# Projections mixed into attention as pairs of 64-row matmuls, with the value sums kept in SBUF between runs

## The chip, the cores and the metric

The kernel runs on one core of one Trainium2 chip, as one program. The metric is the device time of an execution in microseconds (us). PE is TensorE's matmul stream and PEld its weight loads, ACT is ScalarE, DVE is VectorE, POOL is GpSimd, SP issues the DMAs.

## What is computed

Two kinds of layer alternate, twice each, over 2048 tokens of width 576 with 32 heads of width 18:

```python
x = x + _A_ref(_layernorm(x), A_wq, A_wk, A_wv, A_wo)      # softmax attention, one key/value head
x = x + _B_ref(_layernorm(x), B_wqkv, B_w_phi, B_wo)       # linear attention on softmax features
...
# A: q per head, one k and one v for all heads
p = softmax(q @ k.T * Dh**-0.5);  o = p @ v;  return o @ wo
# B: phi = [softmax(t @ w_phi), softmax(-t @ w_phi)] for queries and keys, per head
kv = phi_k.T @ v;  z = phi_k.sum(tokens)
o = (phi_q @ kv) / (phi_q @ z + 1e-6);  return o @ wo
```

## The kernel before

Tokens stand in 16 tiles of 128, in four chunks of four tiles. Products of the projections are made in three parts from values split into a high and a low half (float32r): `PRODUCTS` (L232) lists 14 matmuls for each half of the 576 output columns (`HALF`, 288). `project` (L236) runs these 14 into one PSUM bank; it is a generator that gives way after every second matmul with a weight, and with a negative one after the last.

An attention layer (`attend`, L862) goes through 32 groups, a chunk of 512 queries with four heads each. For each of the 16 key tiles of a group, `score` (L503) makes scores in two *units* of two heads. The 56 rows of queries and keys of two heads lie in the two row halves of the array, so that a unit is a pair of 56-row matmuls (L504) with 512 columns into a score tile of two banks; there are three score tiles. ACT takes the exponential of a unit (L964, 128x1024) into one of nine `pt` tiles. `add_values` (L798) multiplies by the values: four matmuls, in four column strips of 32, per key tile (L800), summed over 16 key tiles in one PSUM bank. When a group is done, `finish_group` (L887) transposes that bank on DVE (`turned`, L889), normalizes (L895, L896), transposes back (L901), splits (L139, L140) and packs into `on` by DMA, in steps.

PSUM has eight banks: six for scores and two *homes* (L879), the tiles `ps` and `acc`. `homes[0]` is the accumulator of the group at hand; the other is `Spare`, in which mixed-in work runs. With each group they change places (L913).

Mixed-in work is the rest of layer A and the start of layer B for a chunk whose attention is done (`chunk_work`, L1206). Per tile: two output projections (`output`, L1048; the sum goes to the residual in `add_residual`, L294), then `flip_tokens` (L639: statistics, normalization and a DVE transpose, written out by DMA), and after the third tile `split_tokens` (L654). Then `mix` (L661) for each tile: two key and two value projections (`keys_values`, L555), two query projections (`queries`, L591), and `update_state` (L575), followed by `feature_end` (L545) for the queries and a block transpose (L632). After a key or query projection `feature_start` (L531) copies the sums to SBUF (L536), takes maximum, minimum and differences on DVE and the exponential on ACT (L543); after a value projection the sums are copied (L567) and `feature_end` follows for the keys. The last chunk's work is done after attention, with other banks (`Banks`, L1075).

The order is set by the loop at L1017. While mixed-in work is there (`bulk`):

```python
sums(scores(BURST))      # three units of scores, then the values that are ready
tick()
ready = scores(BURST)    # three more units
spent = fill()           # mixed-in work up to the next negative weight
in_order()
opens = units[2 * done[0]][1] == 0
if spent < HEAVY and not (spent and opens):
    sums(ready)          # not after a whole projection: that weighs 1750, HEAVY is 1500
tick()
tick()
```

`tick` (L926) takes one step of the finished groups, of the weight loads and of the slow transposes. `in_order` (L948) chains all instructions of PE and DVE in the order in which they were written, so both run exactly in program order. As `fill` stops right behind a projection's last matmul and what is done with its sums, whatever the generator does next (such as `flip_tokens`) is written in the following turn's `fill`, after that turn's values. Without mixed-in work the loop alternates two units and the values of one key tile.

Of the kernel before, what the change touches and what calls it, by code (L numbers as in the profile page):

```python
# [9 lines left out]
F32 = mybir.dt.float32  # L10
# [50 lines left out]
def kernel(ctx, tc, x_in, wq, wk, wv, wo, wqkv, w_phi, wob, out):  # L61
# [174 lines left out]
    def project(dst, w, c0, xs, after=None, products=range(len(PRODUCTS)), last=LASTP):  # L236
        for j, n in enumerate(products):
# [7 lines left out]
            elif j % 2:  # L245
                yield 250

    def run(gen):
        for _ in gen:
            pass  # L250
# [40 lines left out]
        lo_engine.tensor_sub(xs[64:P, 4, :], pb[64:P, :], xs[64:P, 4, :].bitcast(F32))  # L291
        yield -110

    def add_residual(i, b, po):  # L294
        xr = xres[i][:, b * HALF : (b + 1) * HALF]
        V.tensor_add(xr, xr, po)  # L296

    scratch = dram.tile([2, KT * P, D], F32, name="folded")
    flipped = dram.tile([TPC, D, P], F32, name="flipped")
# [228 lines left out]
                for j in range(2):  # L528
                    nc.sync.dma_start(dst[j], mp[:, j, :].bitcast(F32))

    def feature_start(src, e, b, copies):  # L531
        hi = small.tile([P, HH], F32, name="fmax")
        lo = small.tile([P, HH], F32, name="fmin")
        hs = slice(b * HH, (b + 1) * HH)
        if copies is V:
            V.tensor_copy(e[:, hs, 0, :], src)  # L536
# [18 lines left out]
    def keys_values(i, xs, e, st, ps, copies):  # L555
        vb = st["vb"][i % 2]
        for b in range(2):
            po = ps.tile([P, HALF], F32, name="ps")
            yield from project(po, st["wk"], b * HALF, xs, lambda: feature_start(heads(po), e, b, copies))

        def values(po, b):
            dst = vb[:, : H * (DH + 1)].rearrange("p (h d) -> p h d", d=DH + 1)
            dst = dst[:, b * HH : (b + 1) * HH, :DH]
            if copies is A:
                A.activation(dst, heads(po), AF.Copy)
            else:
                V.tensor_copy(dst, heads(po))  # L567
            feature_end(e, b, G if copies is A else V)

        for b in range(2):  # L570
            po = ps.tile([P, HALF], F32, name="ps")
            yield from project(po, st["wv"], b * HALF, xs, lambda: values(po, b))
        return vb

    def update_state(e, vb, st, ps, after=None):  # L575
# [14 lines left out]

    def queries(xs, e, st, ps, copies):  # L591
        for b in range(2):
            po = ps.tile([P, HALF], F32, name="ps")
            yield from project(po, st["wpq"], b * HALF, xs, lambda: feature_start(heads(po), e, b, copies))
        if copies is A:
            for b in range(2):
                feature_end(e, b, G)
# [145 lines left out]
    def read_out(i, pht, st, sp, ps):  # L743
        xo = sp.tile([P, 5 * P], F32, name="xo")
        xv = xo[:, :D].rearrange("p (h d) -> p h d", d=DH)
        for g0, g1 in ((0, 8), (8, NKG)):
            pn = ps.tile([P, 8 * NW], F32, name="ps")
            for g in range(g0, g1):
                hs = KG if g < NKG - 1 else 2
                for t0 in (0, 64):  # L750
                    T.matmul(pn[t0 : t0 + 64, (g - g0) * NW : (g - g0) * NW + hs * (DH + 1)],  # L751
                             pht[: 2 * DH * hs, g, t0 : t0 + 64],
                             st["kvb"][: 2 * DH * hs, g, : hs * (DH + 1)], start=True, stop=True)
            h0, h1 = g0 * KG, min(g1 * KG, H)
            nv = pn[:, : (h1 - h0) * (DH + 1)].rearrange("p (h e) -> p h e", e=DH + 1)
            den = small.tile([P, 24], F32, name="den")
            dv = den[:, : h1 - h0]
            V.tensor_scalar(dv, nv[:, :, DH], 1e-6, None, op0=ALU.add)
            V.reciprocal(dv, dv)
            V.tensor_mul(xv[:, h0:h1, :], nv[:, :, :DH], dv[:, :, None].to_broadcast([P, h1 - h0, DH]))  # L760
        V.tensor_copy(xo[:, D:], xo[:, 512:D])
        yield STAGE
        xs = sp.tile([P, 9, P], F32R, name="xs3")
        yield from transposed(xo, xs, ps, A)
        yield STAGE
        for b in range(2):
            po = ps.tile([P, HALF], F32, name="ps")
            yield from project(po, st["wob"], b * HALF, xs, lambda: add_residual(i, b, po))

    def next_queries(i, stats, layer, st, xpool, sp, ps):  # L770
        p, tt = divmod(i, PAIR)
# [71 lines left out]
    def last_group(acc, on, ps):  # L843
        with tc.high_priority():
            osb = bw.tile([P, 5 * P], F32, name="xn")[:, :CW]
            V.tensor_copy(osb, acc)
# [12 lines left out]
            split(parts[:, 0, :], parts[:, 1, :], osb, V, V)  # L859
            pack(on.bitcast(F32), parts.bitcast(F32), NG - 2)  # L860

    def attend(layer, st, a1o, extra, after_chunk, chunks):  # L862
# [13 lines left out]
        with ctx1:  # L876
# [7 lines left out]
            acc, on = {}, {}  # L884
            urgent, bulk, loads, slow = deque(), deque(), deque(), deque()

            def finish_group(c, g):  # L887
                turned = a1.tile([P, CW], F32, name="turned", bufs=2)
                V.transpose(turned, acc[c, g])  # L889
# [15 lines left out]
                for _ in range(3):  # L905
                    yield STAGE
                if g == NG - 2:
                    bulk.append(after_chunk(c, on[c], Spare(), loads, slow))
                yield STAGE

            def values(c, g, t, pt):
                if t == 0:
                    homes.reverse()  # L913
                    acc[c, g] = bank(*homes[0], [P, CW])
                add_values(acc[c, g], t, [pt[j // 2][:, j % 2, :] for j in range(GH)], t == 0, t == NT - 1)
                if t == NT - 1 and (c, g) == groups[-1]:
                    st["last"] = acc[c, g], on[c]
                elif t == NT - 1:
                    finish(c, g)

            def finish(c, g):
                f = finish_group(c, g)
# [45 lines left out]
            acc[groups[0]] = bank(*homes[0], [P, CW])  # L968
            at[0] = len(spots)
            done[0] = (at[0] - 2 * BURST) // 2  # L970

            def head_values(t, first, last):
                add_values(acc[groups[0]], t, [pts[0, t, j // 2][:, j % 2, :] for j in range(GH)], first, last)

            def head():
                for n, (unit, pt) in enumerate(zip(units, spots)):
# [71 lines left out]
    def output(c, tt, on, wpo, a1o, ps, copies):  # L1048
        xs = on[:, :, tt * P : (tt + 1) * P]
        for b in range(2):  # L1050
            po = ps.tile([P, HALF], F32, name="ps")
            yield from project(po, wpo, b * HALF, xs, lambda: add_residual(c * TPC + tt, b, po))

    def drain(queue):
        while queue:
# [111 lines left out]
    for layer in range(LAYERS):  # L1167
# [3 lines left out]
        with tc.tile_pool(name="a1o", bufs=2) as a1o:  # L1171
# [77 lines left out]
            for i in chunk_tiles(c):  # L1249
                tt = i - c * TPC  # L1250
                for b in range(2):
                    full = (i, b) not in sums
                    po = ps.tile([P, HALF], F32, name="ps") if full else sums[i, b]
                    run(project(po, st["wo"], b * HALF, on[:, :, tt * P : (tt + 1) * P],
                                None, (*EARLY, *LATE) if full else LATE, LATE[-1]))
                    add_residual(i, b, po)
                stats.update(ln_stats([i]))

        st["mixed"] = 0
# [71 lines left out]
```

## Time and profile before

| what | value |
|---|---|
| runs | 2699.45 to 2702.57 us, median of three 2701.58 |
| profiled execution, first to last instruction | 2699.8 us |
| PE busy | 2627.5 us (97%) |
| ACT busy | 2158.1 us (80%) |
| DVE busy | 1213.9 us (45%) |
| granted TensorE clock | 0.994 of full speed |

In the timeline a row gives start and length in us, engine, line, operation, output<-inputs, shape and how many instructions are merged into it; in brackets stands how long the engine was idle before it and what ended that. The groups by line give the count, busy us, the mean ns of one, then the idle time before them. A PE row's length holds the pipeline's latency, so the distance between starts is what one costs. Where a load's wait was over, the first matmul's row starts with its weight load.

### The profile page before, as it was taken

To read this page: it belongs to the slowest core of one execution; us is meant where nothing else is said; L and a number is where in the kernel's file an instruction comes from. 1 tells how busy PE (TensorE), PEld (TensorE's weight loads), DVE (VectorE), ACT (ScalarE), POOL (GpSimd) and SP (SyncE) were. 2 spreads that over 40 slices of the span, in tenths; PEclk is the share of its full clock that TensorE was granted. 3 is DMA by queue.
4 is the path that set the end of the run, shared out by engine and by line. 5 is a ranking of instruction groups with operands and counts; after the bars stand their busy time and mean duration, and the time that the engine had idled before them with its cause. 6 is when DMAs were issued, how large, how long until landed. Compare 5 with 4: busy or idle time off the path is not lost. (4 is left out here: it accounts for less than half of the span.)

```text
span 2699.8 us, 55195 instructions
## 1 busy us (share of the span) xinstructions
PE 2627.5 (97%) x22094; PEld 1444.8 (54%) x22094; DVE 1213.9 (45%) x2807; ACT 2158.1 (80%) x2551; POOL 75.6 (3%) x114
## 2 busy tenths in 40 slices
PE   7999999999999999999999999999999999999999
PEld 6633335453545454558996222455445544554788
DVE  8422244542454245437773111254525452545475
ACT  4599998999899989963335999999998999899421
POOL 1000000000000000002000000000000000000110
PEclk9999999999999999999999999999999999999999
DMA  6531254313421341136645210231224113412354
GB/s 184 163 121 54 65 166 153 93 28 86 119 49 35 84 122 45 38 97 193 185 134 177 71 28 23 55 111 38 58 73 117 41 32 99 118 36 71 108 162 136
DMA packets 353248, 254.30 MB, mean 94 GB/s; under 512 B 191770, under 2 KB 273882, under 8 KB 352986
## 3 DMA queue, kind: packets, MB, share of 16 engines
q1 hardware_dynamic: 352986, 250.71, 32.4%
q8 instruction: 176, 2.88, 0.5%
q14 instruction: 86, 0.70, 0.1%
HBM read 146.12 MB, written 83.69 MB: 85 GB/s over the span
## 5 line engine op out<-in xcount | busy, mean ns | idle before, releaser
L964 ACT ACTIVATE pt<-sc 128x1024 f32<-128x1024 f32 x2036 | 1915.9, 1112 | 155.9 <-PE sc L504 137.2
L504 PE MATMUL sc<-qst,kst 56*128 56x512 f32 x3840 | 712.6, 454 | 16.7 <-ACT pt L964 16.3
L504 PEld LDWEIGHTS sc<-qst,kst 56*128 56x128 f32 x3840 | 324.0, 184 | 618.1 <-ACT pt L964 573.9
L800 PE MATMUL acc<-pt,vst 128*32 128x512 f32 x4096 | 505.1, 599 | 0.0
L800 PE MATMUL ps<-pt,vst 128*32 128x512 f32 x4048 | 491.1, 600 | 1.4 <-DVE featk L536 1.4
L800 PEld LDWEIGHTS ps<-pt,vst 128*32 128x32 f32 x4048 | 105.7, 109 | 212.1 <-issue 206.4
L239 PE MATMUL ps<-wahi,xs 128*128 128x288 f32 x954 | 208.5, 305 | 0.9 <-ACT xs L137 0.7
L800 PEld LDWEIGHTS acc<-pt,vst 128*32 128x32 f32 x4096 | 103.3, 109 | 197.2 <-issue 191.5
L239 PEld LDWEIGHTS ps<-wahi,xs 128*128 128x128 f32 x954 | 157.6, 190 | 11.6 <-issue 3.9
L239 PE MATMUL ps<-walo,xs 128*128 128x288 f32 x530 | 156.2, 297 | 0.0
L889 DVE STREAM_TRANSPOSE turned<-acc 128x512 f32<-128x512 f32 x30 | 21.4, 714 | 217.5 <-PE acc L800 217.5
L388 PE MATMUL ps<-xsc,wbhi 128*128 128x256 f32 x576 | 107.7, 286 | 0.6 <-ACT xsc L137 0.6
L410 ACT ACTIVATE pc<-ps 128x256 fp32r<-128x256 f32 x80 | 30.4, 384 | 93.3 <-PE ps L388 89.2
L239 PEld LDWEIGHTS ps<-walo,xs 128*128 128x128 f32 x530 | 100.6, 190 | 0.0
L263 POOL TENSOR_TENSOR rstd<-var,neghalf 128x1 f32<-128x1 f32 (+1 forms) x56 | 32.0, 571 | 2439.9 <-DVE var L261 2417.7
L137 ACT ACTIVATE xs<-ps 128x512 fp32r<-128x512 f32 x40 | 23.8, 594 | 94.0 <-PE ps L282 93.9
L388 PEld LDWEIGHTS ps<-xsc,wbhi 128*128 128x128 f32 x576 | 91.5, 193 | 1.6 <-ACT xsc L137 1.1
L889 DVE STREAM_TRANSPOSE turned<-ps 128x512 f32<-128x512 f32 x32 | 22.9, 716 | 142.9 <-PE ps L800 142.9
L388 PE MATMUL ps<-xsc,wblo 128*128 128x256 f32 x320 | 86.1, 284 | 0.0
L239 PE MATMUL ps<-wchi,on 128*128 128x288 f32 x378 | 82.2, 303 | 0.0
L296 DVE TENSOR_TENSOR xc<-xc,ps 128x288 f32<-128x288 f32 x58 | 25.7, 445 | 123.4 <-PE ps L239 123.2
L536 DVE COPY featq<-acc 128x288 f32<-128x288 f32 x32 | 14.6, 457 | 123.0 <-PE acc L239 123.0
(257 smaller groups left out, 3200.8 us busy)
## 6 DMA issues: line engine op xcount, KB each, us to landing
qst<-qd SPq DMA_DIRECT2D x360, 72.0 KB
pht<-phi SPq DMA_DIRECT2D x32, 540.0 KB
qd<-pc SPq DMA_DIRECT2D x64, 256.0 KB
on<-parts SPq DMA_DIRECT2D x192, 72.0 KB
phi<-pht SPq DMA_DIRECT2D x96, 144.0 KB
wchi<-wod SPq DMA_DIRECT2D x35, 288.0 KB
wclo<-wod SPq DMA_DIRECT2D x35, 288.0 KB
wchi<-wpqd SPq DMA_DIRECT2D x35, 288.0 KB
```

The source lines that it names most:

```text
L137: A.activation(dst_hi, src, AF.Copy)
L239: T.matmul(dst, xs[:, slot, :], w[half][:, k, c0 : c0 + HALF], start=(n == 0), stop=(n == last))
L263: G.tensor_tensor(rstd, var, neghalf[:, :n], op=ALU.pow)
L296: V.tensor_add(xr, xr, po)
L388: T.matmul(po, lhs, xsc[:, slot, :], start=(n == 0), stop=(n == LASTP))
L410: A.activation(pc[:, 0, :], po, AF.Copy)
L504: T.matmul(sc, kst[head_rows(h), t * P : (t + 1) * P], q[head_rows(h), h // 2, :], start=True, stop=True)
L536: V.tensor_copy(e[:, hs, 0, :], src)
L800: T.matmul(acc[32 * j : 32 * j + 32, :], vst[:, t, :], pts[j], start=first, stop=last)
L889: V.transpose(turned, acc[c, g])
L964: A.activation(pt, sc, AF.Exp, scale=SCALE)
```

## The change

A projection in mixed-in work is made of pairs: for each of the 14 products a matmul over rows 0 to 63 into one bank and one over rows 64 to 127 into another. Both homes are used for this, the accumulator's first. Whoever takes up the sums reads both: a copy or an add of the first half, then an add of the second. So that the accumulator's bank is free, the first `sums` of each turn with mixed-in work ends with its *closing*: DVE copies or adds the bank to an SBUF tile `sum`, and the next values start a new sum in `homes[0]`. This goes on from the first chunk's output on (`started`). A finished group is summed from both places before it is transposed. The projections outside attention stay as they were.

```diff
+    def project_halves(dst, w, c0, xs, after):
+        for n, (slot, half, k) in enumerate(PRODUCTS):
+            for rows, part in ((slice(0, ROWT), dst[0]), (slice(ROWT, P), dst[1])):
+                T.matmul(part, xs[rows, slot, :], w[half][rows, k, c0 : c0 + HALF],
+                         start=(n == 0), stop=(n == LASTP))
+            if n == LASTP:
+                after()
+                yield -250
+            elif n % 2:
+                yield 250
+
+    def projected(ps, w, c0, xs, after):
+        if isinstance(ps, Banks):
+            po = ps.tile([P, HALF], F32, name="ps")
+            return project(po, w, c0, xs, lambda: after((po,)))
+        parts = ps.halves([P, HALF])
+        return project_halves(parts, w, c0, xs, lambda: after(parts))
...
-    def add_residual(i, b, po):
+    def add_residual(i, b, parts):
         xr = xres[i][:, b * HALF : (b + 1) * HALF]
-        V.tensor_add(xr, xr, po)
+        for po in parts:
+            V.tensor_add(xr, xr, po)
+
+    def gathered(dst, parts):
+        V.tensor_copy(dst, heads(parts[0]))
+        for po in parts[1:]:
+            V.tensor_add(dst, dst, heads(po))
...
         if copies is V:
-            V.tensor_copy(e[:, hs, 0, :], src)
             src = e[:, hs, 0, :]
+            gathered(src, parts)
+        else:
+            src = heads(parts[0])
...
-                V.tensor_copy(dst, heads(po))
+                gathered(dst, parts)
...
+                def halves(self, shape):
+                    return [bank(*home, shape) for home in homes]
...
             def finish_group(c, g):
                 turned = a1.tile([P, CW], F32, name="turned", bufs=2)
-                V.transpose(turned, acc[c, g])
+                a = acc.pop((c, g))
+                if a["sum"] is not None:
+                    V.tensor_add(a["sum"], a["sum"], a["bank"])
+                V.transpose(turned, a["bank"] if a["sum"] is None else a["sum"])
...
-            def values(c, g, t, pt):
+            def values(c, g, t, pt, closing):
                 if t == 0:
                     homes.reverse()
-                    acc[c, g] = bank(*homes[0], [P, CW])
-                add_values(acc[c, g], t, [pt[j // 2][:, j % 2, :] for j in range(GH)], t == 0, t == NT - 1)
-                if t == NT - 1 and (c, g) == groups[-1]:
-                    st["last"] = acc[c, g], on[c]
+                    acc[c, g] = {"bank": None, "sum": None}
+                a = acc[c, g]
+                opened = a["bank"] is None
+                if opened:
+                    a["bank"] = bank(*homes[0], [P, CW])
+                add_values(a["bank"], t, [pt[j // 2][:, j % 2, :] for j in range(GH)],
+                           opened, closing or t == NT - 1)
+                last = (c, g) == groups[-1]
+                if t == NT - 1 and last:
+                    st["last"] = a, on[c]
+                    closing = bool(bulk)
                 elif t == NT - 1:
                     finish(c, g)
+                    closing = False
+                if closing:
+                    if a["sum"] is None:
+                        a["sum"] = a1o.tile([P, CW], F32, name="sum", bufs=2)
+                        V.tensor_copy(a["sum"], a["bank"])
+                    else:
+                        V.tensor_add(a["sum"], a["sum"], a["bank"])
+                    a["bank"] = None
...
-            def sums(until):
+            def sums(until, close=False):
                 while done[0] < until:
                     n, t, _ = units[2 * done[0]]
-                    values(*groups[n], t, [pts.pop((n, t, hh)) for hh in range(2)])
+                    values(*groups[n], t, [pts.pop((n, t, hh)) for hh in range(2)],
+                           close and done[0] == until - 1)
                     done[0] += 1
                     in_order()
...
                 if bulk:
-                    sums(scores(BURST))
+                    sums(scores(BURST), started[0])
                     tick()
```

More of the change, by code (lines that the diff above doesn't have):

```diff
@@ L529, in exact_maxima, with feature_start @@
                     nc.sync.dma_start(dst[j], mp[:, j, :].bitcast(F32))
-    def feature_start(src, e, b, copies):
+    def feature_start(parts, e, b, copies):
         hi = small.tile([P, HH], F32, name="fmax")
@@ L557, in keys_values, with values @@
         for b in range(2):
-            po = ps.tile([P, HALF], F32, name="ps")
-            yield from project(po, st["wk"], b * HALF, xs, lambda: feature_start(heads(po), e, b, copies))
-        def values(po, b):
+            yield from projected(ps, st["wk"], b * HALF, xs, lambda parts: feature_start(parts, e, b, copies))
+        def values(parts, b):
             dst = vb[:, : H * (DH + 1)].rearrange("p (h d) -> p h d", d=DH + 1)
@@ L564, in values @@
             if copies is A:
-                A.activation(dst, heads(po), AF.Copy)
+                A.activation(dst, heads(parts[0]), AF.Copy)
             else:
-                V.tensor_copy(dst, heads(po))
+                gathered(dst, parts)
             feature_end(e, b, G if copies is A else V)
         for b in range(2):
-            po = ps.tile([P, HALF], F32, name="ps")
-            yield from project(po, st["wv"], b * HALF, xs, lambda: values(po, b))
+            yield from projected(ps, st["wv"], b * HALF, xs, lambda parts: values(parts, b))
         return vb
@@ L592, in queries @@
         for b in range(2):
-            po = ps.tile([P, HALF], F32, name="ps")
-            yield from project(po, st["wpq"], b * HALF, xs, lambda: feature_start(heads(po), e, b, copies))
+            yield from projected(ps, st["wpq"], b * HALF, xs, lambda parts: feature_start(parts, e, b, copies))
         if copies is A:
@@ L766, in read_out @@
         for b in range(2):
-            po = ps.tile([P, HALF], F32, name="ps")
-            yield from project(po, st["wob"], b * HALF, xs, lambda: add_residual(i, b, po))
+            yield from projected(ps, st["wob"], b * HALF, xs, lambda parts: add_residual(i, b, parts))
     def next_queries(i, stats, layer, st, xpool, sp, ps):
@@ L845, in last_group @@
             osb = bw.tile([P, 5 * P], F32, name="xn")[:, :CW]
-            V.tensor_copy(osb, acc)
+            if acc["sum"] is None or acc["bank"] is None:
+                V.tensor_copy(osb, acc["bank"] or acc["sum"])
+            else:
+                V.tensor_add(osb, acc["sum"], acc["bank"])
             po = ps.tile([P, TPC, P], F32, name="ps")
@@ L883, in tile @@
                     return bank(*homes[1], shape)
-            acc, on = {}, {}
+                def halves(self, shape):
+                    return [bank(*home, shape) for home in homes]
+            acc, on, started = {}, {}, [False]
             urgent, bulk, loads, slow = deque(), deque(), deque(), deque()
@@ L907, in finish_group @@
                 if g == NG - 2:
+                    started[0] = True
                     bulk.append(after_chunk(c, on[c], Spare(), loads, slow))
                 yield STAGE
-            def values(c, g, t, pt):
+            def values(c, g, t, pt, closing):
                 if t == 0:
                     homes.reverse()
-                    acc[c, g] = bank(*homes[0], [P, CW])
-                add_values(acc[c, g], t, [pt[j // 2][:, j % 2, :] for j in range(GH)], t == 0, t == NT - 1)
-                if t == NT - 1 and (c, g) == groups[-1]:
-                    st["last"] = acc[c, g], on[c]
+                    acc[c, g] = {"bank": None, "sum": None}
[9 more added lines that the diff above has]
+                    closing = bool(bulk)
                 elif t == NT - 1:
                     finish(c, g)
+                    closing = False
[3 more added lines that the diff above has]
+                        V.tensor_copy(a["sum"], a["bank"])
+                    else:
+                        V.tensor_add(a["sum"], a["sum"], a["bank"])
+                    a["bank"] = None
             def finish(c, g):
@@ L967, in attend @@
             spots = [*st["head"], *(a1.tile([P, 2, 512], F32, name="pt", bufs=3 * BURST) for _ in range(2 * BURST))]
-            acc[groups[0]] = bank(*homes[0], [P, CW])
+            acc[groups[0]] = {"bank": bank(*homes[0], [P, CW]), "sum": None}
             at[0] = len(spots)
@@ L972, in head_values @@
             def head_values(t, first, last):
-                add_values(acc[groups[0]], t, [pts[0, t, j // 2][:, j % 2, :] for j in range(GH)], first, last)
+                add_values(acc[groups[0]]["bank"], t, [pts[0, t, j // 2][:, j % 2, :] for j in range(GH)], first, last)
             def head():
@@ L1050, in output @@
         for b in range(2):
-            po = ps.tile([P, HALF], F32, name="ps")
-            yield from project(po, wpo, b * HALF, xs, lambda: add_residual(c * TPC + tt, b, po))
+            yield from projected(ps, wpo, b * HALF, xs, lambda parts: add_residual(c * TPC + tt, b, parts))
     def drain(queue):
@@ L1255 @@
                                 None, (*EARLY, *LATE) if full else LATE, LATE[-1]))
-                    add_residual(i, b, po)
+                    add_residual(i, b, (po,))
                 stats.update(ln_stats([i]))
```

## The prediction

> **What bounds the kernel now.** I read the page first, then the stretches of the span, then the timeline of one turn of the loop in which projections are mixed into attention, then the vector engine's own timeline around the places where it has much to do.
>
> ```profile
> span 2699.8 us, 55195 instructions
> ...
> PE 2627.5 (97%) x22094; PEld 1444.8 (54%) x22094; DVE 1213.9 (45%) x2807; ACT 2158.1 (80%) x2551; POOL 75.6 (3%) x114
> ```
>
> ```profile
> 400.00:700.00 300.00, 295.94 (x2418) 145.85 (x2419) 136.42 (x278) 271.66 (x294) 3.25 (x6) 1.00 0.32 89
> ...
> 1500.00:1700.00 200.00, 200.00 (x1316) 57.71 (x1308) 24.45 (x42) 200.00 (x220) 0.00 (x0) 1.00 0.10 26
> ```
>
> The page calls PE busy for 97%, which invites one to shorten PE's work. The stretches (columns: length, then PE, PEld, DVE, ACT, POOL busy, PE clock, DMA) say more. Without mixed-in work (1500 to 1700) ACT is busy all the time. With it (400 to 700) neither PE nor ACT is full: each waits for the other somewhere. So I follow one turn.
>
> ```profile
> 605.66 0.96 PE L504 MATMUL sc<-qst,kst 56*128 56x512 f32 x6
> 606.26 5.82 ACT L964 ACTIVATE pt<-sc 128x1024 f32<-128x1024 f32 x6 [0.27 <-PE sc L504]
> 606.55 0.19 PEld L239 LDWEIGHTS acc<-wchi,xs 128*128 128x128 f32 x1 [0.36 <-issue]
> 608.60 1.07 PE L504 MATMUL sc<-qst,kst 56*128 56x512 f32 x6
> 608.71 0.46 DVE L536 COPY featq<-acc 128x288 f32<-128x288 f32 x1 [4.35 <-PE acc L239]
> 609.17 0.19 PEld L504 LDWEIGHTS sc<-qst,kst 56*128 56x128 f32 x2 [0.27 <-ACT pt L964]
> 609.60 2.78 PE L800 MATMUL ps<-pt,vst 128*32 128x512 f32 x24
> 612.31 0.96 PE L504 MATMUL sc<-qst,kst 56*128 56x512 f32 x6
> 612.45 0.72 DVE L889 STREAM_TRANSPOSE turned<-ps 128x512 f32<-128x512 f32 x1 [1.45 <-PE ps L800]
> ```
>
> ```profile
> 608.09 1.03 ACT L964 ACTIVATE pt<-sc 128x1024 f32<-128x1024 f32 x1
> ```
>
> A turn is: a burst of three score pairs (605.66), the projection (606.55), a second burst (608.60), a run of values (609.60), and the next turn's first burst at 612.31: 6.65 us. Take the first burst as time 0. Its first exponential starts at 0.60 and the third at 2.43 (608.09); the third ends 1.03 later, at 3.46, and only then has the second burst's third pair a free score tile: its load is at 3.51 (609.17), and that row says it waited 0.27 for ACT. The values follow at 3.94, the next burst at 6.65. This closed loop runs through ACT, one score pair and the values. **The projection is not in it.** PE's own work is 0.89 + 2.05 + 0.89 + 2.71 = 6.54 a turn (the second burst without a wait takes 0.89, below), 0.11 less than the loop. A turn without a feature exponential shows the same length, with ACT idle for longer:
>
> ```profile
> 501.33 5.82 ACT L964 ACTIVATE pt<-sc 128x1024 f32<-128x1024 f32 x6 [0.84 <-PE sc L504]
> ...
> 507.99 1.94 ACT L964 ACTIVATE pt<-sc 128x1024 f32<-128x1024 f32 x2 [0.83 <-PE sc L504]
> ```
>
> That the projection has 0.11 to spare and no more can be tested on a turn in which it was late:
>
> ```profile
> 439.90 0.96 PE L504 MATMUL sc<-qst,kst 56*128 56x512 f32 x6
> 442.26 0.40 PE L239 MATMUL acc<-wahi,xs 128*128 128x288 f32 x1 [1.40 <-DVE turned L889]
> 444.32 0.96 PE L504 MATMUL sc<-qst,kst 56*128 56x512 f32 x6
> 445.21 2.78 PE L800 MATMUL ps<-pt,vst 128*32 128x512 f32 x24
> 447.93 0.97 PE L504 MATMUL sc<-qst,kst 56*128 56x512 f32 x6
> ```
>
> It started at 2.36 instead of 0.89, 1.47 late, and the turn took 8.03, 1.38 more. So what is late beyond the slack is paid in full.
>
> **The change part by part. The row halves.** The 192 mixed-in projections (2 layers, 3 chunks, 4 tiles, 8 each) go from 14 full matmuls to 14 pairs in the form in which the scores run. I take a pair to cost what a full product costs now, 0.13 us, because the score pairs, also in the two halves, come 0.23 apart (606.00 to 606.23 below) with 512 columns, and a full product at its rate of 0.134 for 288 columns would need 0.238 for 512: both matmuls of a pair run at once. What goes is the change of form between scores and projection:
>
> ```profile
> 606.00 0.39 PE L504 MATMUL sc<-qst,kst 56*128 56x512 f32 x2
> ```
>
> ```profile
> 606.23 0.40 PE L504 MATMUL sc<-qst,kst 56*128 56x512 f32 x2
> ```
>
> ```profile
> 606.79 0.29 PE L239 MATMUL acc<-wclo,xs 128*128 128x288 f32 x1
> ```
>
> ```profile
> 608.38 0.29 PE L239 MATMUL acc<-wclo,xs 128*128 128x288 f32 x1
> 608.60 0.30 PEld L504 LDWEIGHTS sc<-qst,kst 56*128 56x128 f32 x4 [0.16 <-issue]
> ```
>
> The last pair streams from 606.23 to 606.46; the second product is at 606.79, so the first streamed from 606.66: 0.20 lost. The last product ends at 608.38 + 0.13 = 608.51 and the next pair, loaded at 608.60, streams a load (0.11) later, at 608.71: 0.20 again. So 0.4 us of PE per turn, 192 x 0.4 = 77 us if PE were the bound. By the loop above it is worth nothing in a plain turn: the third pair of the second burst still waits for the exponential. It only raises the projection's slack, and only by the second half, since the first is taken back by the closing read. The slack becomes about 0.28: the pairs end at 0.9 + 0.11 + 14 x 0.134 = 2.89, the third pair could stream two pairs later, at 3.34, and is free at 3.62.
> [...]
>
> **The closing read.** Both banks are now needed for the two halves. After each run of values in these turns DVE moves the accumulator to SBUF, and the projection waits for it.
>
> ```profile
> L140 DVE TENSOR_TENSOR xs<-ps,xs 128x512 fp32r<-128x512 f32 x40 | 27.1, 679 | 9.7 <-ACT xs L137 9.2
> ```
>
> DVE starts 0.14 after the values (612.31 to 612.45 above), 0.68 for 512 columns from PSUM, 0.06 to PE: 0.88. The projection starts at 0.89 now, so with DVE free this costs nothing. DVE runs in its written order, so the cover is gone where other work stands ahead of it.
>
> **The second wait, which is the costly one.** The next run of values opens anew in the bank of the first half, so it waits for DVE's copy of that half. In a plain turn the copy runs from 3.05 to 3.51 (608.71 above) and the values start at 3.94: nothing. But the closing read stands in DVE's order ahead of whatever the next projection's generator writes first, and that now starts at 0.84, not when the previous projection ended:
>
> ```profile
> 403.35 0.81 DVE L258 BATCH_NORM_STATS2 bnst<-xc 128x6 f32<-128x288 f32 x2
> ...
> 406.07 0.78 DVE L632 STREAM_TRANSPOSE pht<-featq 128x576 f32<-128x576 f32 x1
> ...
> 416.63 0.81 DVE L258 BATCH_NORM_STATS2 bnst<-xc 128x6 f32<-128x288 f32 x2
> ...
> 421.31 0.29 DVE L658 TENSOR_TENSOR xs<-xn,xs 64x128 fp32r<-64x128 f32 x1
> ```
>
> ```profile
> 480.07 0.75 DVE L548 TENSOR_REDUCE fz<-featq 128x32 f32<-128x576 f32 x1
> ...
> 483.87 1.38 DVE L632 STREAM_TRANSPOSE pht<-featq 128x1152 f32<-128x1152 f32 x1
> ```
>
> - Turning a token tile (L640 to L644): 3.50 long. DVE reaches the copy at 0.84 + 3.50 + 0.04 = 4.38, copy 0.46, to PE 0.06: the values start at 4.90 instead of 3.94. **+0.95**, three times a chunk.
> - The same with the split of the next tokens (416.63 to 421.60, 4.97): 6.37, **+2.4**, once a chunk.
> - Ending the query features and their transpose (480.07 to 485.25, 5.18) before the next tile's first key projection: 6.58, **+2.6**, three times a chunk.
>
> Per chunk 3 x 0.95 + 2.4 + 3 x 2.6 = 13.1; six chunks, **78 us**. Here the values are late, so all of it is paid.
>
> **Finished groups.** A group that ends during mixing puts 0.68 (its last sum) in front of its transposition, and later its second part
>
> ```profile
> 614.46 0.70 DVE L901 STREAM_TRANSPOSE osb<-turned 128x512 f32<-128x512 f32 x1
> ...
> 615.66 0.69 DVE L140 TENSOR_TENSOR parts<-osb,parts 128x512 fp32r<-128x512 f32 x1
> ```
>
> 1.9 us, stands between a projection's features and the next closing read. Features now begin at 3.05 with copy and a second read (0.46 + 0.45, the only other new DVE work), and last until 5.85; then 1.9: 7.75, whereas the closing read is due at 6.79. The projection is 0.9 late, minus 0.28 of slack: 0.6; up to 1.1 where the group ends within a run. I count 22 such ends in the DVE timeline, at 0.8: 18 us. Four more meet a turned tile (0.68 + 0.72 + 0.25 + 0.69 in front of it: 1.7 each) and six the start of a chunk's mixing (about 1 each): 13 us. Bounds for these 31: 0, if each falls into a wait that is there anyway, and 55.
>
> **Sum:** 0 + 78 + 31 = 109 on the span of 2699.8: 2809. The median of the runs, 2701.58, is 1.8 above that span, so **2811 us**. The second reads' 0.45 on DVE is otherwise hidden by its idle time (DVE 136 of 300 busy); the extra 0.68 outside mixed turns is nothing, as there ACT is the bound.
>
> **The rivals.**
> - **Faster:** the loop is not as closed as I read it, and the 0.4 comes off each of the 150 plain turns (192 less the 42 with late values), while the late ones fit into waits: 2701 - 60 = 2640. The place is the third pair's wait at 609.17; it decides if that wait shrinks when the projection ends sooner. For it: PE is busy 97%, and 6.54 is only 0.11 below the loop. Against it: that wait is for the exponential, which does not move. Chance 0.11. With the 78 on top of this gain, or a part of both, it ends within 0.2% (about what a measurement of this kernel can tell from no change): 0.04.
> - **The change does not do what it says:** the halves run one after the other. A projection then takes 28 x 0.134, 1.88 longer, less the 0.28: 1.6 in each of 168 turns, 2.4 to 2.6 in the others, so 2701 + 269 + 61 + 15 = about 3045. Against it: the score pairs, 0.23 apart with 512 columns. Chance 0.05.
> - **Slower, as summed:** 0.80, in a range of 2755 (two thirds of the 78 and no group ends) to 2875 (78, 55 and some 40 for the first chunk's weight splits on DVE and for knock-on).
> The range of 2745 to 2880 leaves out the faster, the equal and the far case, 0.2 together. Faster 0.11, same 0.04, slower 0.85.
>
> **What would show it.** Right: plain turns still take 6.65, the load at L504 still waits for ACT, and the loads of the values (L800) now wait for DVE's copies (L536, L296) by 1 to 2.6 us some 42 times; the scores follow the projection without the 0.16 of issue. Wrong: plain turns of 6.3, or pairs more than 0.15 apart, or DVE doing a token tile's turning ahead of the closing read.

## The result and the profile after

The changed kernel takes **2833.84 us** (median of four runs, 2832.79 to 2834.96) against 2701.1 (2699.45 to 2702.57, four runs): a ratio of 1.0493, interval 1.0478 to 1.0508. The prediction said 2811, in a range of 2745 to 2880.

First the page of the profile after, its span, its busy engines and the strip of the granted clock:

```profile
span 2833.2 us, 61212 instructions
...
PE 2649.1 (94%) x24782; PEld 1449.0 (51%) x24782; DVE 1465.9 (52%) x3253; ACT 2145.6 (76%) x2551; POOL 75.8 (3%) x114
...
PEclk9999999999999999999999999999999999999999
```

DVE has 252 us more work, the closings and the second reads among it; PE is busy 22 us more and ACT no more. The span is 133.4 longer. So what was added isn't work of the two full engines. Where PE's time goes, the groups by line of the values say, two from before and two from after; the last columns are busy time, the mean of one, and the idle time before the group with what ended it:

```profile
L800 PE MATMUL acc<-pt,vst 128*32 128x512 f32 x4096 | 505.1, 599 | 0.0
L800 PE MATMUL ps<-pt,vst 128*32 128x512 f32 x4048 | 491.1, 600 | 1.4 <-DVE featk L536 1.4
```

```profile
L822 PE MATMUL acc<-pt,vst 128*32 128x512 f32 x4096 | 520.5, 616 | 52.5 <-DVE featk L318 30.4 <-DVE xc L315 20.0 <-DVE sum L963 1.7
L822 PE MATMUL ps<-pt,vst 128*32 128x512 f32 x4048 | 503.2, 613 | 23.8 <-DVE featk L318 13.9 <-DVE xc L315 4.9 <-DVE featk L320 3.9
```

The values waited 1.4 us before and 76 after, 69 of it for two instructions: DVE's copy of a projection's first half (L318) and the residual's first add (L315). That is the prediction's *second wait*. And the same number of matmuls is busy for 27.5 us longer, more than PE's whole 22; what that is comes below.

**A plain turn.** In the timeline after (start, length, engine, line, operation; in brackets the idle time before it and what ended it; here and below only chosen rows are shown):

```profile
559.06 0.97 PE L528 MATMUL sc<-qst,kst 56*128 56x512 f32 x6
559.20 0.69 DVE L965 TENSOR_TENSOR sum<-sum,ps 128x512 f32<-128x512 f32 x1 [1.06 <-PE ps L822]
559.94 0.18 PEld L251 LDWEIGHTS ps<-wbhi,xs 64*128 64x128 f32 x1 [0.35 <-DVE sum L965]
561.78 0.32 PEld L528 LDWEIGHTS sc<-qst,kst 56*128 56x128 f32 x4
...
562.57 0.18 PEld L528 LDWEIGHTS sc<-qst,kst 56*128 56x128 f32 x2 [0.47 <-ACT pt L1011]
563.01 1.07 PE L822 MATMUL ps<-pt,vst 128*32 128x512 f32 x8
565.72 0.97 PE L528 MATMUL sc<-qst,kst 56*128 56x512 f32 x6
```

The turn is 6.66 long, as before. The closing read (559.20) ends in time for the projection (559.94). The projection ends earlier, and the next scores' loads have no issue gap in front of them (561.78). But the third pair waits for the same exponential, 0.47 instead of 0.27 (562.57), and the values stand where they stood, at 3.95. What PE saves has become waiting.

**A late turn**, with the end of the query features in front of the copy:

```profile
492.89 0.96 PE L528 MATMUL sc<-qst,kst 56*128 56x512 f32 x6
493.03 0.69 DVE L965 TENSOR_TENSOR sum<-sum,acc 128x512 f32<-128x512 f32 x1
493.63 0.75 DVE L574 TENSOR_REDUCE fz<-featq 128x32 f32<-128x576 f32 x1
...
497.44 1.38 DVE L655 STREAM_TRANSPOSE pht<-featq 128x1152 f32<-128x1152 f32 x1
498.74 0.42 DVE L318 COPY featk<-acc 128x288 f32<-128x288 f32 x1
499.22 4.33 PE L822 MATMUL acc<-pt,vst 128*32 128x512 f32 x24 [2.31 <-DVE featk L318]
...
503.47 1.07 PE L528 MATMUL sc<-qst,kst 56*128 56x512 f32 x6
```

DVE begins the features at 0.74 of the turn, behind the closing read, and comes to the copy at 498.74; PE has stood for 2.31 us. The values start at 6.33 instead of 3.94. Then something that no part of the prediction has: the run of values takes 4.25 us (499.22 to 503.47), not 2.71. The same wait, one tile later, has no such sequel:

```profile
549.52 2.78 PE L822 MATMUL ps<-pt,vst 128*32 128x512 f32 x24 [2.30 <-DVE featk L318]
```

The stretches tell why. Their columns are length, then PE, PEld, DVE, ACT and POOL busy, and then the granted clock:

```profile
496.90:500.31 3.41, 1.10 (x14) 0.42 (x16) 3.24 (x6) 2.20 (x3) 0.00 (x0) 1.00 0.27 55
500.31:503.73 3.42, 3.42 (x18) 0.69 (x12) 1.32 (x4) 0.68 (x1) 0.00 (x0) 0.50 0.93 142
544.69:548.10 3.41, 2.50 (x30) 1.74 (x26) 3.24 (x6) 3.41 (x5) 0.00 (x0) 1.00 0.00 0
548.10:551.51 3.41, 1.99 (x20) 0.68 (x24) 3.20 (x7) 1.31 (x2) 0.00 (x0) 1.00 0.49 85
```

From 500.31 to 503.73 TensorE had half its clock (0.50). The strip of the page, at 71 us a digit, can't show this; its mean over the span, 0.982 against 0.994 before, can.

**Where the 133 us went.** From the starts of scores, projection and values in each of the 192 turns, after minus before, and the same for five experiments below (us in all, count of turns in brackets):

| | after | e1 | e2 | e4 | e6 | e7 |
|---|---|---|---|---|---|---|
| values late: feature endings (18) | 42.9 | 0.0 | 42.9 | 42.8 | 0.0 | 6.0 |
| values late: tile turned and tokens split (5) | 11.9 | 0.0 | 11.9 | 11.9 | 0.0 | 0.0 |
| values late: tile turned (15) | 14.2 | 1.4 | 10.2 | 14.2 | 0.8 | 0.8 |
| first 13 turns of the first chunk | 11.6 | 6.4 | 11.2 | 12.5 | 9.0 | 11.6 |
| projection late | 22.8 | 4.4 | 15.9 | 23.4 | 23.3 | 2.9 |
| all other turns | 0.1 | 6.2 | −1.5 | −0.5 | 3.7 | 5.8 |
| values run longer than 2.71 | 28.8 | 6.0 | 19.2 | 9.8 | 0.3 | 0.3 |
| sum | 132.3 | 24.5 | 109.8 | 114.3 | 37.1 | 27.4 |

The sum is within 1.1 us of the growth of the span for the change, and within 4.1 (e1) for the experiments. In the column "after", 107 other turns add nothing.

### The profile page after: what moved, and what is told of

The parts are those of the page before. It is cut to its first block, busy times and chain, and to the rows that moved or that the text cites. A ratio compares the mean times of both kernels' runs of the same rounds, so it can differ in the third digit from the quotient of the medians.

```text
span 2833.2 us, 61212 instructions
## 1 busy us (share of the span) xinstructions
PE 2649.1 (94%) x24782; PEld 1449.0 (51%) x24782; DVE 1465.9 (52%) x3253; ACT 2145.6 (76%) x2551; POOL 75.8 (3%) x114
## 5 line engine op out<-in xcount | busy, mean ns | idle before, releaser
L239 PE MATMUL ps<-wahi,xs 128*128 128x288 f32 x720 | 155.0, 302 | 1.7 <-ACT xs L137 1.7
L965 DVE TENSOR_TENSOR sum<-sum,acc 128x512 f32<-128x512 f32 x74 | 50.9, 688 | 114.3 <-PE acc L822 114.1
L251 PE MATMUL ps<-wahi,xs 64*128 64x288 f32 x432 | 98.9, 311 | 10.9 <-DVE sum L963 10.9
L965 DVE TENSOR_TENSOR sum<-sum,ps 128x512 f32<-128x512 f32 x86 | 59.1, 687 | 89.3 <-PE ps L822 89.3
L251 PE MATMUL ps<-wbhi,xs 64*128 64x288 f32 x432 | 95.8, 304 | 9.9 <-DVE sum L965 8.8
L251 PE MATMUL ps<-wchi,xs 64*128 64x288 f32 x432 | 95.8, 304 | 4.4 <-DVE sum L963 2.4
L251 PE MATMUL acc<-wchi,xs 64*128 64x288 f32 x432 | 95.7, 304 | 4.2 <-DVE sum L965 4.2
L251 PE MATMUL acc<-wahi,xs 64*128 64x288 f32 x432 | 98.9, 311 | 0.0
L251 PE MATMUL acc<-wbhi,xs 64*128 64x288 f32 x432 | 95.7, 304 | 2.4 <-DVE sum L963 2.4
L251 PE MATMUL ps<-wchi,on 64*128 64x288 f32 x432 | 95.7, 304 | 0.8 <-DVE sum L963 0.8
```

Source lines behind the costliest of these rows:

```text
L239: T.matmul(dst, xs[:, slot, :], w[half][:, k, c0 : c0 + HALF], start=(n == 0), stop=(n == last))
L251: T.matmul(part, xs[rows, slot, :], w[half][rows, k, c0 : c0 + HALF], start=(n == 0), stop=(n == LASTP))
L965: V.tensor_add(a["sum"], a["sum"], a["bank"])
```

## The experiments

**The theory** after the result: nothing is lost in the projections themselves. Between a projection and the next values now stands a read by DVE, in an order that puts a closing and other long work ahead of it, and half a clock window, 1.7 us, is paid on top after many of the places where PE stood. **Rivals:** the row halves themselves cost time; the closings cost it by keeping DVE busy; PE's own work is the bound of the plain turn, and the gain of the halves is hidden behind other losses.

**e1: the closings alone.** Projections are whole matmuls in the spare bank, as before.

```diff
-        parts = ps.halves([P, HALF])
-        return project_halves(parts, w, c0, xs, lambda: after(parts))
+        po = ps.tile([P, HALF], F32, name="ps")
+        return project(po, w, c0, xs, lambda: after((po,)))
```

> The changed kernel with only one of its parts: the values are closed into SBUF each turn, but a mixed-in projection is 14 whole matmuls into the spare bank, as before the change. Theory (the loss comes from the values waiting for DVE's copy of the first half, behind DVE work that the closing read now pushes back): the values reopen a bank that only the closing read holds, 0.88 us after the run, and the copy has until the next projection; so the time of the kernel before, 2698 to 2710 us. Rival 'the closing reads cost by themselves': about 160 of 0.69 us on the path, 2800 or more. Rival 'the row halves cost': also about 2701, told apart by the next kernel.

Measured: 2722.0, ratio 1.008 (1.0063 to 1.0097). The closings by themselves do not cost the 133; the late values of feature endings are gone. But the expectation had too little: some 21 us are left. The timeline of e1, from a turn's first burst to its values, shows one part of it, which the table has under "all other turns":

```profile
819.15 0.97 PE L528 MATMUL sc<-qst,kst 56*128 56x512 f32 x6
819.75 1.03 ACT L1011 ACTIVATE pt<-sc 128x1024 f32<-128x1024 f32 x1 [0.84 <-PE sc L528]
820.14 0.46 DVE L567 TENSOR_TENSOR featk<-featk,fmax 128x288 f32<-128x288 f32 x1
820.68 0.67 ACT L569 ACTIVATE featk<-featk 128x576 f32<-128x576 f32 x1
821.25 3.76 ACT L1011 ACTIVATE pt<-sc 128x1024 f32<-128x1024 f32 x4
...
823.67 2.78 PE L822 MATMUL ps<-pt,vst 128*32 128x512 f32 x24
```

DVE reached the features of the first key half late (820.14), so their exponential on ACT (820.68) fell between two exponentials of scores (819.75 and 821.25); the values are at 4.52 instead of 3.94. Here the closing's cost is passed on through ACT's order, not through PE's wait.

**e2: whole matmuls, but in the accumulator's bank.** No row halves and one read; the one thing left of the halves is that the projection stands in the bank that the next values need.

```diff
-        parts = ps.halves([P, HALF])
-        return project_halves(parts, w, c0, xs, lambda: after(parts))
+        po = ps.halves([P, HALF])[0]
+        return project(po, w, c0, xs, lambda: after((po,)))
...
-                    return [bank(*home, shape) for home in homes]
+                    return [bank(*home, shape) for home in homes[:1]]
```

> The changed kernel without row halves: 14 whole matmuls into one bank, the one that the closing read has just freed, and one read of the sums. Theory (the bank and DVE's order make the loss): all waits stay, the projection's slack is 0.11 instead of 0.28 us a turn, the second read's 0.49 us is gone: 2815 to 2850 us. Rival 'the row halves cost, on PE': the loss goes with them, about 2701.

Measured: 2812.52, ratio 1.042 (1.0403 to 1.0438), a little under the range. In its timeline, a feature ending:

```profile
832.15 0.97 PE L528 MATMUL sc<-qst,kst 56*128 56x512 f32 x6
...
838.00 0.42 DVE L318 COPY featk<-ps 128x288 f32<-128x288 f32 x1
838.47 2.78 PE L822 MATMUL ps<-pt,vst 128*32 128x512 f32 x24 [2.31 <-DVE featk L318]
```

The same 2.31 of waiting, the same 6.32. Of the change's 133 us, 112 are there without a single row half. What the halves add is 21: the residual's add and the late projections (their second read), and more half-clock windows. No group of turns in the table shows a gain of the halves.

**e3: the accumulator's bank holds the second half.** It is read last, so each run of values waits for two reads.

```diff
-                    return [bank(*home, shape) for home in homes]
+                    return [bank(*home, shape) for home in homes[::-1]]
```

> The changed kernel with the two banks of a projection exchanged: the half that is read first lies in the other bank, so the accumulator's bank is read last. Theory: the values start when the second read is done instead of the first, 0.49 us later in the 42 or so turns that wait already, and 0.1 to 0.15 us late in the plain turns, which do not wait now: 2834 + 21 + 12 to 20, so 2860 to 2880 us, a plain turn 6.75 to 6.8 us. Rival 'the values do not wait for the copy but for something else': 2834.

Measured: 2873.85, ratio 1.0639 (1.0621 to 1.0657), in the expected range. Now the wait has reached the plain turn too:

```profile
892.94 0.96 PE L528 MATMUL sc<-qst,kst 56*128 56x512 f32 x6
...
896.42 0.45 DVE L320 TENSOR_TENSOR featq<-featq,acc 128x288 f32<-128x288 f32 x1
896.92 2.78 PE L822 MATMUL acc<-pt,vst 128*32 128x512 f32 x24
899.64 0.96 PE L528 MATMUL sc<-qst,kst 56*128 56x512 f32 x6
```

The values stand right behind the second read, at 3.98, and the turn takes 6.70. The theory's quantity, the end of the read of the bank in question, moved by one read (0.45 and the gap ahead of it) and the values with it: a feature ending's values went from 6.32 to 6.88. The plain turn grew by 0.05 only, less than the 0.1 to 0.15 expected. That the time fell into the range all the same is luck: against the kernel after, the runs of values at half clock add 14 us, which the expectation didn't have. PE now stands for 2.86 us or more ahead of the values of a feature ending, and all 18 of these runs are long (4.05 to 4.41), where 11 were.

**e4: more work for PE.** In the 18 turns with a feature ending, the last product's pair is made 16 times more (the text on record calls it the 13th), 2.1 us of PE work in a turn where PE had stood 2.3.

```diff
+            if n == LASTP:
+                for _ in range(again):           # 16 in the first key projection of a chunk's tiles 2 to 4
+                    for rows, part in ((slice(0, ROWT), dst[0]), (slice(ROWT, P), dst[1])):
+                        T.matmul(part, xs[rows, slot, :], w[half][rows, k, c0 : c0 + HALF],
+                                 start=False, stop=False)
```

> The changed kernel with more work for PE: in the first key projection of each chunk's tiles 2 to 4 the 13th product is added 16 more times (so those sums hold it too often), 2.1 us of matmuls in 18 turns in which PE idles 2.3 us before the values. Theory 'PE's idle time lets the granted clock fall in the run of values behind it (4.4 instead of 2.71 us in 18 turns of the trace, 11 of them here)': the idle time is nearly filled, the values start when they did, and they run at full clock: 2834 less 11 x 1.7, about 2815 us. Rival 'PE is the bound': 18 x 2.1 more, 2872. Rival 'the clock falls anyway': 2834.

Measured: 2813.01, ratio 1.0418 (1.04 to 1.0435): 18 times 2.1 us of work more, 21 us less time. The timeline, and the stretch of the values with its clock:

```profile
836.35 0.97 PE L533 MATMUL sc<-qst,kst 56*128 56x512 f32 x6
...
842.67 2.78 PE L828 MATMUL ps<-pt,vst 128*32 128x512 f32 x24 [0.47 <-DVE featk L323]
845.38 0.96 PE L533 MATMUL sc<-qst,kst 56*128 56x512 f32 x6
```

```profile
842.60:845.40 2.80, 2.73 (x26) 0.70 (x26) 2.20 (x6) 2.45 (x4) 0.00 (x0) 1.00 0.94 154
```

The values are as late as in the changed kernel (6.32), but all 18 runs take 2.71 at full clock. So the longer runs of values come from PE standing still, not from the values or their data; what is left of that term, 9.8, lies in seven turns without a feature ending.

**e5: less work for PE, in the kernel before.** Three of the 14 products of a mixed-in projection are left out.

```diff
+    FEWER = [n for n in range(len(PRODUCTS)) if n not in (7, 8, 9)]
...
+                               range(len(PRODUCTS)) if isinstance(ps, Banks) else FEWER)
```

> The kernel before, with three of the 14 products left out of each mixed-in projection (those sums are incomplete): 0.40 us of PE less in each of 192 turns, as much as the change of form between scores and projection costs. Theory (the loop runs over the exponentials, the third score pair and the values, and the projection is not in it): nothing, 2695 to 2703 us, a plain turn still 6.65 us. Rival 'PE, 97% busy, is the bound': 192 x 0.40 = 77 us less, 2624.

Measured: 2699.34 against 2700.65, ratio 0.9995 (0.9986 to 1.0004). Nothing, for the same 0.40 us of PE a turn that the change was to save, and more than 40 us of PE's busy time, as the page of e5 has it:

```profile
PE 2584.8 (96%) x21518; PEld 1369.7 (51%) x21518; DVE 1214.3 (45%) x2807; ACT 2137.6 (79%) x2551; POOL 75.6 (3%) x114
```

```profile
801.31 0.97 PE L506 MATMUL sc<-qst,kst 56*128 56x512 f32 x6
...
804.82 0.19 PEld L506 LDWEIGHTS sc<-qst,kst 56*128 56x128 f32 x2 [0.65 <-ACT pt L969]
...
807.96 0.97 PE L506 MATMUL sc<-qst,kst 56*128 56x512 f32 x6
```

The timeline says where it went: the third pair waits 0.65 instead of 0.27. This has none of the change's new waits, so the rival "PE bounds the plain turn" falls, busy 97% or not.

**e6: DVE's long work spread.** The changed kernel, with a token tile's normalization written right behind its second output projection, and the feature ending cut in three pieces, one ahead of each of the next tile's first three projections.

```diff
+            if todo:                   # in keys_values, keys and values: one piece of the last tile's ending
+                todo.pop(0)()
...
+            st["todo"] = [lambda eq=eq: feature_end(eq, 0, V), lambda eq=eq: feature_end(eq, 1, V), turned_features]
...
+            add_residual(c * TPC + tt, b, parts)
+            if b == 1:
+                norm_tokens(c * TPC + tt)
```

> The changed kernel with DVE's work spread: the statistics and normalization of a token tile are written right behind its last output projection, ahead of the next closing read; the two endings of the query features and their transpose go singly in front of the next tile's first three projections. Theory (DVE work between the closing read and the copy delays the values): the 75 us of the turns with turned tiles or feature endings go, and most of the 29 us at low clock behind them; the 29 us around finished groups stay: 2725 to 2750. Rival 'the waits are not of DVE's order': 2834.

Measured: 2737.42, ratio 1.0134 (1.0118 to 1.015), as expected. Late values go from 69 (the first three rows of the table) to 0.8 and the longer runs from 28.8 to 0.3: 96 of the 133 us were the order of DVE's work. The late projections stay at 23.

**e7: e6, and a finished group's second part kept out of a projection's back.** It is written only behind the closing read.

```diff
-                while c - 1 in on and c - 1 not in st["added"]:
+                while (c - 1 in on and c - 1 not in st["added"]) or not early[0]:
                     yield STAGE
...
                     sums(scores(BURST), started[0])
                     tick()
+                    early[0] = False
...
                     tick()
                     tick()
+                    early[0] = True
```

> As the kernel with DVE's work spread, and the second part of a finished group (transpose, split) is written only behind a closing read, not in front of the next. Theory: most of the rest goes too, and what is left is the loop of the kernel before, with its plain turn of 6.65 us: 2700 to 2720, not below 2697. Rival 'without the waits the gain of the row halves shows': 0.2 to 0.4 us a turn, 2625 to 2665.

Measured: 2727.5, ratio 1.0099 (1.0085 to 1.0113), 7 above the range. The late projections fall from 23.3 to 2.9, so that term was the finished groups. But six of the us come back in the feature endings, where the group's second part (DVE L948) now stands ahead of the same copy:

```profile
490.40 0.96 PE L528 MATMUL sc<-qst,kst 56*128 56x512 f32 x6
491.14 0.70 DVE L948 STREAM_TRANSPOSE osb<-turned 128x512 f32<-128x512 f32 x1
...
494.80 0.45 DVE L318 COPY featk<-acc 128x288 f32<-128x288 f32 x1
495.30 2.78 PE L838 MATMUL acc<-pt,vst 128*32 128x512 f32 x24 [0.89 <-DVE featk L318]
```

And with most waits gone, 131 of the 192 turns take 6.65 or 6.66 and none less than 6.64: no gain of the halves comes to light.

**e8 and e9: the other side of the loop.** In the kernel before, the exponentials of mixed-in turns take 448 of 512 columns; e9 leaves out e5's three products as well.

```diff
+                cols = slice(0, 448) if bulk and mixing[0] else slice(0, 512)
+                A.activation(pt[:, :, cols], sc[:, :, cols], AF.Exp, scale=SCALE)
+                if cols.stop < 512:
+                    G.memset(pt[:, :, cols.stop :], 1.0)
```

> The kernel before, with shorter exponentials while mixed-in work is there after the first chunk: of the 2 x 512 columns of a unit 2 x 448 are done, the rest is set to 1 by POOL (so that part of the attention is not computed). About 0.11 us less for each exponential, three of which are in the loop. Theory: a plain turn falls from 6.65 us, by less than the 0.33, to PE's own 6.54; 0.11 in some 170 turns, and 0.11 for each of the 144 exponentials of the turns without a projection, which ACT bounds: 2701 - 18 - 16 = about 2667 us. Rival 'PE is the bound of a turn': only the 16, 2685. Rival 'ACT's own work is the bound': 0.66 a turn, about 2560.

> Both: the shorter exponentials, and 11 of 14 products in each mixed-in projection (neither the attention nor those sums are complete). Theory: PE's own turn is 6.14 us now, so the loop's full 0.33 shows, a plain turn is 6.32 us, though the products alone gave nothing: 2701 - 192 x 0.33 - 16 = about 2622 us. Rival 'the exponentials alone set the turn': as with the shorter exponentials alone.

Measured: e8 2672.89, ratio 0.9902 (0.9886 to 0.9919), 6 above what was expected; e9 2635.07, ratio 0.9762 (0.9746 to 0.9779), 13 above what was expected. An exponential of 896 columns takes 0.92 to 0.93 in the timeline of e8, against 1.03 for the 1024 of before, so the 0.11 expected was about right. In the timeline of e8 the six loads of the second burst are in one row, which waits for no exponential; in e9, in the loads of the second burst's third pair (807.65), the wait is back:

```profile
814.45 0.97 PE L504 MATMUL sc<-qst,kst 56*128 56x512 f32 x6
...
817.41 0.53 PEld L504 LDWEIGHTS sc<-qst,kst 56*128 56x128 f32 x6 [0.17 <-issue]
```

```profile
804.44 0.97 PE L506 MATMUL sc<-qst,kst 56*128 56x512 f32 x6
...
807.65 0.19 PEld L506 LDWEIGHTS sc<-qst,kst 56*128 56x128 f32 x2 [0.37 <-ACT pt L972]
...
810.79 0.97 PE L506 MATMUL sc<-qst,kst 56*128 56x512 f32 x6
```

A plain turn in the four kernels: 6.65 before, 6.66 with fewer products, 6.57 with shorter exponentials, 6.36 with both. Each alone gains 0.08 or nothing, both together 0.29. The loop through ACT and PE's own 6.54 lie side by side, as the prediction read them, and a change to one of them is worth 0.1 us a turn at most.

## Why the prediction was right, and where it was not

- **Plain turns: 0 predicted, 0.1 us measured over 107 turns.** The loop is closed through ACT; e5 and e8 show it without the change's waits.
- **A pair of halves costs one product, 0.13 us:** so it is. In the timeline after, two pairs in succession, both matmuls of each within 0.01:

```profile
494.01 0.29 PE L251 MATMUL acc<-walo,xs 64*128 64x288 f32 x1
494.01 0.29 PE L251 MATMUL ps<-walo,xs 64*128 64x288 f32 x1
494.14 0.29 PE L251 MATMUL acc<-wahi,xs 64*128 64x288 f32 x1
494.15 0.29 PE L251 MATMUL ps<-wahi,xs 64*128 64x288 f32 x1
```

  Each row is 0.29 long, and the next pair starts 0.13 later. The far rival (halves one after another) falls with these rows. Nor is anything lost behind the last pair: the next scores start 0.13 after it (561.78 to 561.91).
- **Late values: 78 predicted, 74.7 measured.** The 18 feature endings come to +2.38 each (+2.6 predicted), the six turns with flip and split to +2.38 (+2.4), the 18 turned tiles to +0.97 (+0.95): 12 of these are an output projection's, 1.0 each, and six a key projection's, 0.92 each in the mean, but twelve of the 18 come to 0.68 to 0.76 only, and in five of the other six DVE has steps of a finished group in the same turn. So a turned tile by itself was sized too high, and that the mean meets the forecast is luck. (The table has five and fifteen of these, as the first chunk's are in its fourth row.) The cause is shown: e1 takes the bank away and e6 the order, and either removes nearly all of it; e3 lengthens it.
- **Finished groups and the first chunk: 31 predicted, 29 measured** (what is left of the sum when late values and longer runs are taken off). e7 shows the groups' part, 20 of 23 in the late projections. But some 5 of the 29 are half clock as well, as in three turns it fell on a late projection: the one that starts at 1043.71, after a wait of 2.45, takes 3.52 to the next scores, and the one at 1846.82, after a wait of 2.44 but at full clock, takes 1.96. The waits alone come to about 24.
- **The step that failed: "Here the values are late, so all of it is paid."** What is late was paid once by the delay and a second time by the clock. In 18 turns the values ran longer, by 1.6 us in the mean, 28.8 us that no term of the sum had, and that is why 109 became 133: 3.3 less on the late values, 2 less on the groups, 28.8 more here, 1 outside the turns. PE stood still for 1.8 to 2.5 us ahead of these runs or of the turn's projection, and in the 192 turns of before its longest wait was 1.40 (in the turn at 439.90); e4 shows that the standing is the cause, and e6 that without it the term is 0.3. The time lies in the range because of room that was given to other things, group ends of up to 55 and 40 for splits and knock-on.
- **The rival "faster" (2640):** its deciding sign was the third pair's wait at L504 shrinking. It grew, from 0.27 to 0.47.

What stays open: 24.5 us of e1 and 27.4 of e7 are traced to turns, and by the timeline to features that reach ACT late and to work that the first chunk's start piles on DVE; no run took these causes away one by one.

## What to carry to other kernels

Before shortening the engine that is busy 97%, look for the loop that sets the turn's length: here 0.40 us of PE a turn was worth nothing by itself, shorter exponentials by themselves 0.08, and both together 0.29. A PSUM bank that two uses shared tied the second use here to whoever reads the first, in that engine's written order (late values at feature endings cost 42.9 us in e2, 0.0 in e1): list what stands ahead of the read, turn by turn, and move that before you share the bank. And price a PE wait like the 2.3 us here by more than its length: it was followed by a window at half clock in 11 cases of 18.

## What the runs showed of the hardware

**Half the clock for 3.41 us, after a stretch in which PE stood.** In the clock record of the trace after, 22 of 26 falls last 3.41 us, all at half the clock (0.50), and the starts lie whole multiples of 3.413 us apart (those at 397.91 and 500.31 are 30 apart). The windows don't follow the work. The rows of the two late turns above are such windows: PE stood 2.31 of the 3.41 from 496.90 on, and the next window had half the clock; the other wait, as long, was cut by a window's border in 0.91 and 1.42, and nothing fell. It is so in all 18 feature endings: in the 11 with 2.30 us or more of standing inside one window the next was at half clock, in the seven with 2.04 or less it was not. At half clock a window of values costs 3.41 / 2 = 1.7 us, which is what the longer runs show (2.71 + 1.7 = 4.41, the commonest length of a longer run). The border isn't sharp elsewhere: over the whole trace falls followed windows with as little as 1.67 of standing (1258.07 to 1261.48). In e3, where PE stands for 2.86 or more, all 18 were followed by a fall.
